# Other DMA engines and smaller pieces for the 352 uneven rows of `w_out` in a memory-bound decode kernel

## The chip, the cores and the metric

The kernel runs on one core of a Trainium2 chip. The metric is the device time of one execution in microseconds; three runs of the kernel before the change gave 663.13, 663.26 and 663.29 us, a median of 663.26 us.

## What is computed

One decode step for four sequences: a layer norm, attention over a cache of 4096 keys and values in 32 heads of 128, and beside it a gated MLP (gMLP) that reads the same normed input. Cut to what matters:

```
xn  = layernorm(x)                                   # (4, 1, 640)
q   = xn @ wq                                        # wq 640 x 4096, 32 heads of 128
o   = softmax(q k^T / sqrt(128)) v                   # k, v: 4 x 32 x 4096 x 128, bf16
A   = o @ wo                                         # wo 4096 x 640
z   = gelu(xn @ w_in)                                # w_in 640 x 1728
g   = w_sp * layernorm(z[864:]) + b_sp
B   = (z[:864] * g) @ w_out                          # w_out 864 x 640
out = x + A + B
```

The two caches are 134 MB each, and all other tensors together 14 MB; nearly everything the kernel does is to read the caches once.

## The kernel before

**The stream.** All big loads are DMAs issued by the sync engine (SP) in the order in which they stand in the program: `wq` (L111), `w_in` (L114), the first 512 rows of `w_out` (L118), the other 352 rows of `w_out` in four DMAs (L128), then 16 units of keys and 16 units of values (L167, 8 MB each, some cut in two), and between and behind them `wo` (L175). A unit is 128 partitions x 64 KB. The units are placed in five slots of one big tile `kv`; a load into a slot waits until the engines that read the slot's last content are done. A DMA of 128 partitions is spread over the core's 16 DMA engines, eight partitions to each. Each engine has its own queue and works it off in order.

**The 352 rows.** 864 rows of `w_out` are 512 + 352. The 512 go four to a partition over all 128 partitions (`w_out`, FA = 4). The 352 are put into `w_rest`, nine chunks (FR = 9) of up to 44 partitions. The table `RB` has an entry for each DMA: the quarter of 32 partitions, the first chunk, a number of engines `ni`, and a number of rows per partition `n`. A DMA gets 4 x `ni` partitions with `n` consecutive rows of 1280 B in each. Its source is written with the dimension `ni` outermost, and so it runs on `ni` DMA engines: 8 and 5 for the first quarter, 3 and 3 for the second. In rows per engine that is 68 on engines 0 to 2, 32 on engines 3 and 4, 28 on engines 5 to 7, none on 8 to 15.

**Semaphores of DMAs.** The framework gives the DMAs that SP and ACT issue eight semaphores in turn, in program order: the three small loads of ACT (L105, L107, L108) and SP's own share them. A DMA that gets a semaphore which an earlier DMA used waits, on the issuing engine, until that earlier DMA has landed whole. The eight are called HW0 to HW7 here.

**The MLP.** After `w_in` has landed, TensorE computes `z` (L309 for the 512 rows' part, L312 for the rest, one matmul for each quarter and each of DC = 5 chunks), ACT applies gelu (L318, and L322 with two instructions for each entry of `RB`), a short chain over DVE, POOL and ACT makes the gated vector `uT` (L353), and 26 matmuls at L367 multiply it with `w_out` and `w_rest`.

**The attention.** For each eighth of a key unit, DVE transposes 128 x 2048 words into a tile `kT` (L389, two buffers in turn, from the pool `ktpool`) and TensorE makes scores from it (L400). The two buffers of `ktpool` first hold `w_rest`, so the first transposes wait for the matmuls of L367. After the softmax, values are multiplied at L474. The end is a projection with `wo` (L517) whose last pieces are loaded last, one sum on DVE (L580), and the store of the result (L583).

Of the kernel before, what the change touches and what calls it, by code (L numbers as in the profile page):

```python
# [11 lines left out]
F32 = mybir.dt.float32  # L12
BF16 = mybir.dt.bfloat16
# [3 lines left out]
def kernel(  # L17
# [19 lines left out]
    nc = tc.nc  # L37
    P = 128
    B, Sq, D = A_x.shape
    _, H, Sk, Dh = A_k_cache.shape  # L40
# [4 lines left out]
    NE = HG // HP  # L45
    M = P // HG
    T = Sk // M
    C2 = 2
    TC = 32
# [6 lines left out]
    Fh = F2 // 2  # L56
    FA = 4
    FR = 9
    RB = ((0, 0, 8, 7), (0, 7, 5, 1), (1, 0, 3, 7), (1, 7, 3, 2))
    NRP = 44  # L60
    assert Fh == FA * P + 4 * sum(i * c for _, _, i, c in RB)
    FC = FA + FR
    NOUT = A_wo.shape[1]
    NH = 2
    NO2 = NOUT // NH
# [3 lines left out]
    const = ctx.enter_context(tc.tile_pool(name="const", bufs=1))  # L69
    small = ctx.enter_context(tc.tile_pool(name="small", bufs=2))  # L70

    NKT = max(2 * TC * 32, 7 * NOUT // 2)
    ktpool = ctx.enter_context(tc.tile_pool(name="ktpool", bufs=2))
    ppool = ctx.enter_context(tc.tile_pool(name="ppool", bufs=2))
    ps_s = ctx.enter_context(tc.tile_pool(name="ps_s", bufs=1, space=bass.MemoryType.PSUM))
    ps_o = ctx.enter_context(tc.tile_pool(name="ps_o", bufs=2, space=bass.MemoryType.PSUM))
# [6 lines left out]
    def misc_ps(shape, dtype):  # L83
        misc_ctr[0] += 1
        return ps_m.tile(shape, dtype, tag="misc", name=f"misc{misc_ctr[0]}")


    SL = T * Dh // 2
    kv = const.tile([P, 5 * SL], BF16)

    def at_slot(i, n, off=0):
        return kv[:, i * SL + off:i * SL + off + n]
# [20 lines left out]
    w_in = at_slot(2, n_in).rearrange("p (c f) -> p c f", c=DC)  # L113
    nc.sync.dma_start(out=w_in, in_=B_w_in.rearrange("(p c) f -> p c f", c=DC))  # L114

    nf = FA * P
    w_out = at_slot(2, FA * NOUT, n_in).rearrange("p (c n) -> p c n", c=FA)
    nc.sync.dma_start(out=w_out, in_=B_w_out[0:nf, :].rearrange("(p c) n -> p c n", p=P))  # L118
    w_rest = []
    for k, n in ((0, 7), (1, 2)):  # L120
        t = ktpool.tile([P, NKT], F32, tag="kT", name=f"w_rest{k}")[:NRP].bitcast(BF16)[:, 0:n * NOUT]
        w_rest.append(t.rearrange("p (c n) -> p c n", c=n))
    nc.gpsimd.memset(w_rest[1].rearrange("p c n -> p (c n)").bitcast(F32), 0.0)
    r_at = [nf]
    for q, c0, ni, n in RB:
        r_at.append(r_at[-1] + 4 * ni * n)
        k = c0 // 7
        nc.sync.dma_start(out=w_rest[k][32 * q:32 * q + 4 * ni, 0:n].rearrange("p c n -> p (c n)"),  # L128
                          in_=B_w_out[r_at[-2]:r_at[-1], :].rearrange("(r i c) n -> i r (c n)", r=4, c=n))

    NB = 32 * FC
    z_at = n_in + FA * NOUT
# [19 lines left out]
    def unit(item, t0, t1):  # L152

        s0, s1 = place[item]
        assert s1 == s0 + 1 or t1 <= T // 2 or t0 >= T // 2
        if t0 >= T // 2:
            return at_slot(s1, (t1 - t0) * Dh, t0 * Dh - SL)
        return at_slot(s0, (t1 - t0) * Dh, t0 * Dh)
# [91 lines left out]
    for q in range(4):  # L250
        nc.gpsimd.tensor_copy(out=SelE[32 * q:32 * q + 32, :, q % 2, :],
                              in_=b8[32 * q:32 * q + 32, 8:8 + HP, None].to_broadcast((32, HP, P // HG)))
# [10 lines left out]
                          in_=ident_f[:].rearrange("p (q x c) -> p q x c", q=2, c=C2))  # L263
# [10 lines left out]
    proj = ps_j.tile([64, 512], F32)  # L274
    RW = NH * B
    for hf in range(NH):
        nc.tensor.matmul(proj[0:32, 0:NO2], lhsT=ident_bf[:XR, 1 - hf:33 - hf],
                         rhs=x_bf[:, hf * NO2:(hf + 1) * NO2], start=(hf == 0), stop=False)
# [4 lines left out]
    for hf in range(2):  # L283
        for c in range(DC):
            for j in range(NG):
                n0 = j * HG * Dh + hf * 512
                nc.tensor.matmul(q4_ps[32 * j:32 * j + 32, hf * 512:hf * 512 + 512], lhsT=xnT[:, c, :],  # L287
                                 rhs=wq[:, c, n0:n0 + 512], start=(c == 0), stop=(c == DC - 1))
# [13 lines left out]

    w_z = w_in.rearrange("p c (a f) -> p c a f", a=2)
    z_ps = misc_ps([P, 2, FA, 32], F32)
    zr_ps = misc_ps([64, 2, 256], F32)
    w_za = w_z[:, :, :, 0:nf].rearrange("p c a (q j i) -> p c q a i j", q=4, j=32)
    for c in range(DC):
        for q in range(4):
            nc.tensor.matmul(z_ps[32 * q:32 * q + 32], lhsT=xnT[:, c, :], rhs=w_za[:, c, q], start=(c == 0), stop=(c == DC - 1))  # L309
        for q in range(2):  # L310
            f0, f1 = r_at[2 * q], r_at[2 * q + 2]
            nc.tensor.matmul(zr_ps[32 * q:32 * q + 32, :, 0:f1 - f0], lhsT=xnT[:, c, :],  # L312
                             rhs=w_z[:, c, :, f0:f1], start=(c == 0), stop=(c == DC - 1))
    z_f = at_slot(2, 2 * 3 * NB, z_at).bitcast(F32).rearrange("p (a n) -> p a n", a=3)
    z_b = at_slot(2, 2 * NB, z_at + 6 * NB).rearrange("p (a n) -> p a n", a=2)
    zT = z_f[:, 0:2, :].rearrange("p a (i j) -> p a i j", j=32)
    nc.gpsimd.memset(z_f[:, 0:2, :], 0.0)
    nc.scalar.activation(out=zT[:, :, 0:FA, :], in_=z_ps[:], func=ACT.Gelu_apprx_tanh)  # L318
    for (q, c0, ni, n), f0, f1 in zip(RB, r_at[:-1], r_at[1:]):
        f0, f1 = f0 - r_at[2 * q], f1 - r_at[2 * q]  # L320
        for a in range(2):
            nc.scalar.activation(out=zT[32 * q:32 * q + 32, a, FA + c0:FA + c0 + n, 0:4 * ni].rearrange("p c (i r) -> p c i r", r=4),  # L322
                                 in_=zr_ps[32 * q:32 * q + 32, a, f0:f1].rearrange("p (r i c) -> p c i r", r=4, c=n),
                                 func=ACT.Gelu_apprx_tanh)

    one_bf = const.tile([1, P], BF16)
# [27 lines left out]
    uT = z_b[:, 1, :]  # L354
# [6 lines left out]
    for f0 in range(0, FC, 4):  # L361
        for hf in range(NH):
            for fc in range(f0, min(f0 + 4, FC)):
                n = P if fc < FA else NRP
                nb = 32 if fc == 1 and hf == 0 else RW
                u0, r0 = 32 * fc + 1 - hf, 32 * (fc % 2)
                nc.tensor.matmul(proj[r0:r0 + nb, 0:NO2], lhsT=uT[:n, u0:u0 + nb],  # L367
                                 rhs=(w_out[:, fc] if fc < FA else w_rest[(fc - FA) // 7][:, (fc - FA) % 7])[:, hf * NO2:(hf + 1) * NO2],
                                 start=(fc == 1 and hf == 0), stop=False)


# [9 lines left out]
    def emit_K(u, k):  # L381

        g, b = divmod(u, B)
        hh = first.get(u, 0) ^ (k // 4)
        qp, kh = k // 2 % 2, k % 2
        t0 = 2 * TC * (2 * hh + qp)
        kw = unit(("k", u), t0, t0 + 2 * TC).bitcast(F32).rearrange("p (t w) -> p t w", w=KW)[:, :, 32 * kh:32 * kh + 32]
        kT = ktpool.tile([P, NKT], F32, tag="kT", name="kT")[:, 0:2 * TC * 32]
        nc.vector.transpose(kT[:].rearrange("p (t r) -> p t r", r=32), kw)  # L389
        if ("S", g) not in state:  # L390
            S_new = ps_s.tile([P, 2, TC, M], F32, tag="S", name="S")
            state[("S", g)] = S_new
        S_ps = state[("S", g)]
        kb = kT[:].bitcast(BF16).rearrange("p (i t e m w) -> p i t e m w", i=2, e=NE, m=M, w=2)
        w0 = 8 - (b * C2 + hh)
        for w in range(2):
            for i in range(2):
                for e in range(NE):
                    q = 2 * qp + e
                    nc.tensor.matmul(S_ps[32 * q:32 * q + 32, i], lhsT=QZ[:, b, 2 * kh + w, e, w0:w0 + 32],  # L400
                                     rhs=kb[:, i, :, e, :, w], start=(b == 0 and k < 4 and kh == 0 and w == 0),
                                     stop=(b == B - 1 and k >= 4 and kh == 1 and w == 1))
# [124 lines left out]
    for i, item in enumerate(seq):  # L527
        if i + 1 < len(seq):
            key, u = seq[i + 1]
            load_unit(seq[i + 1])  # L530
            if key == "k" and u == 2 * B - 1:
                load_wo(u // B - 1)
        else:
            load_wo(NG - 3)
            load_wo(NG - 2)
            load_wo(NG - 1, (0, 4, 6, 7, 8))
        key, u = item
        g, b = divmod(u, B)
        if key == "k":
            done = b == B - 1 and g > 0  # L540
            for k in range(8):
                emit_K(u, k)
                if done and k == 1:
                    emit_sel(g - 1)
                if done and k == 2:
                    emit_oT(g - 1)
                if done and k == 5 and g == 1:
                    emit_proj(g - 1)
            if b == B - 1:
                if g < NG - 1:  # L550
                    fill_qz(g + 1)
                softmax(g)
        else:
            emit_V(u)
# [6 lines left out]
    for c, hf in ((0, 0), (1, 0), (0, 1), (1, 1), (2, 0), (2, 1)):  # L561
        p = min(c, 1)
# [49 lines left out]
```

## Time and profile before

| | |
|---|---|
| median of three runs | 663.26 us |
| profiled execution, span from first to last instruction | 661.2 us |
| outside the span (median less span) | 2.0 us |
| bytes read from HBM | 282.24 MB, 427 GB/s over the span |
| busy: PE, DVE, ACT, POOL | 287.5, 372.2, 73.6, 67.0 us |
| chain that ended last: DMA, DVE, PE | 77%, 9%, 4% |
| packets on SP's queue (q1) | 6879, 99.0% of 16 engines' span |
| instruction packets on q8 | 17, 0.28 MB |

The page gives the profiled execution's span; the run's own time is 2.0 us longer because of what lies around the first and the last instruction. "DMA" shares are means over 16 engines. "SPq" rows are SP's queue: the time it took to issue a DMA, with the wait ahead of it where several are merged in one row. The trace also keeps each DMA packet with its start, length and size, though not the number of its engine.

### The profile page before, as it was taken

The page shows a single profiled execution, that of the slowest core. Times are in us where ns is not written, and L with a number is a line of the kernel's source. Part 1 is how long each engine was busy: PE and PEld are TensorE (multiplying, and loading weights), DVE is VectorE, ACT ScalarE, POOL GpSimd, SP SyncE. Part 2 cuts the span into 40 slices and gives each one's busy share as a digit, 9 for nine tenths or more (in the row PEclk, how much of TensorE's full clock was granted, in tenths as well). Part 3 has the DMA queues.
Part 4 walks back from the last instruction along what each step waited for, and adds up shares of the span by engine and source line. Part 5 has one row for each costly group of instructions (what it writes and reads, how often), then busy time and mean ns, then how long its engine had stood idle before and what let it go on. Part 6 is the DMA issues. An engine that isn't in the chain of part 4 may idle for free.

```text
span 661.2 us, 5415 instructions
## 1 busy us (share of the span) xinstructions
PE 287.5 (43%) x2247; PEld 106.6 (16%) x2247; DVE 372.2 (56%) x306; ACT 73.6 (11%) x145; POOL 67.0 (10%) x137
## 2 busy tenths in 40 slices
PE   0436656446062555235436065533706244551236
PEld 0211212112011121111112022110202112120113
DVE  2229999766191759718356286764629175971112
ACT  0300000341100000430200000070110000043200
POOL 3600000031200000130300000030110000003300
PEclk9857788669577587676758577875858769766678
DMA  9999999999999999999999999999999999999996
GB/s 372 452 446 420 420 447 438 429 444 417 436 436 433 428 425 437 433 436 445 416 432 433 432 421 450 427 432 429 437 440 433 424 433 416 445 444 429 419 420 285
DMA packets 6930, 282.58 MB, mean 427 GB/s; under 512 B 811, under 2 KB 1091, under 8 KB 1487
## 3 DMA queue, kind: packets, MB, share of 16 engines
q1 hardware_dynamic: 6879, 282.24, 99.0%
q8 instruction: 17, 0.28, 0.2%
q14 instruction: 6, 0.05, 0.0%
q10 hardware_dynamic: 28, 0.01, 0.0%
HBM read 282.24 MB, written 0.01 MB: 427 GB/s over the span
## 4 chain that ended last, share of the span: by engine, by line
DMA 77%; DVE 9%; issue 8%; PE 4%; ACT 0%; SPq 0%; DVEq 0%; ACTq 0%
DMA kv<-in_A_k_cache_dram 46%; DMA kv<-in_A_v_cache_dram 26%; DVE kT L389 8%; PE O L474 4%; DMA kv<-in_A_wo_dram 4%; DMA kv<-in_A_wq_dram 2%; DVE pT_t L456 0%; ACT Zb L437 0%; DVE m L407 0%; ACT p_bf L450 0%; PE S L400 0%; PE misc L411 0%; SPq L128 0%; PE proj L517 0%; DVE o_q L569 0%
## 5 line engine op out<-in xcount | busy, mean ns | idle before, releaser
L389 DVE STREAM_TRANSPOSE kT<-kv 128x2048 f32<-128x2048 f32 x128 | 282.8, 2275 | 128.1 <-DMA kv<-in_A_k_cache_dram 128.1
L400 PE MATMUL S<-kT,QZ 128*32 128x512 bf16 x1024 | 187.1, 498 | 261.9 <-DVE kT L389 261.9
L400 PEld LDWEIGHTS <-QZ 128*32 128x32 bf16 x1024 | 59.8, 110 | 387.5 <-issue 323.2
L474 PE MATMUL O<-kv,Zb 128*32 128x512 bf16 x1024 | 75.0, 458 | 56.4 <-DMA kv<-in_A_v_cache_dram 49.5
L437 ACT ACTIVATE Zb<-pT_t,MkE 32x128 bf16<-32x128 bf16 x120 | 60.8, 507 | 117.6 <-PE O L474 104.6
L483 DVE TENSOR_TENSOR om<-O,Mk 128x512 f32<-128x512 f32 x15 | 10.4, 692 | 93.8 <-PE O L474 93.8
L435 POOL TENSOR_SCALAR Zb<-pT_t,MkE 32x128 bf16<-32x128 bf16 x60 | 43.1, 718 | 138.6 <-PE O L474 126.1
L474 PEld LDWEIGHTS <-Zb 128*32 128x32 bf16 x1024 | 34.0, 113 | 97.3 <-issue 69.6
L450 ACT ACTIVATE p_bf<-S,negmax 128x1024 bf16<-128x1024 f32 x4 | 4.5, 1115 | 403.7 <-DVE negmax L417 403.7
L433 DVE TENSOR_SCALAR Zb<-pT_t,MkE 32x128 bf16<-32x128 bf16 x76 | 25.1, 330 | 2.3
L375 POOL COPY QZ<-qT 32x32 bf16<-32x32 bf16 x16 | 5.0, 315 | 188.9 <-PE S L400 188.4
L484 DVE TENSOR_REDUCE R<-om 128x128 f32<-128x512 f32 x15 | 15.3, 1021 | 0.5
L456 DVE STREAM_TRANSPOSE pT_t<-p_bf 128x1024 bf16<-128x1024 bf16 (+1 forms) x8 | 9.6, 1240 | 5.5 <-ACT p_bf L450 5.5
L461 POOL TENSOR_SCALAR rs<-MkB,rowsum 128x4 f32<-128x4 f32 x4 | 1.2, 299 | 112.7 <-ACT p_bf L450 112.7
L507 POOL MEMSET oT<- 128x66 bf16 x4 | 0.5, 146 | 96.6 <-PE proj L517 96.6
L407 DVE TENSOR_REDUCE m<-S 128x1 f32<-128x1024 f32 x4 | 4.9, 1224 | 6.0 <-PE S L400 6.0
L486 DVE TENSOR_SCALAR R<-O,Mk 128x128 f32<-128x128 f32 x1 | 0.3, 350 | 14.0 <-PE O L474 14.0
L496 PE MATMUL misc<-R,SelX 128*128 128x512 f32 x8 | 4.5, 644 | 7.2 <-DVE R L484 5.5
L287 PE MATMUL q<-kv,xnT 128*32 128x512 bf16 x40 | 4.3, 614 | 6.4 <-DVE xnT L208 6.4
L463 PE MATMUL misc<-rs,SelE 128*128 128x4 f32 x8 | 2.4, 365 | 10.4 <-POOL rs L461 10.4
L191 DVE CAST kv<-kv 8x640 f32<-8x640 bf16 x1 | 0.5, 482 | 10.7 <-DMA kv<-in_A_x_dram 10.7
L499 DVE TENSOR_TENSOR om<-misc,h 128x512 f32<-128x512 f32 x4 | 2.8, 692 | 4.9 <-PE misc L496 4.9
(102 smaller groups left out, 80.0 us busy)
## 6 DMA issues: line engine op xcount, KB each, us to landing
kv<-in_A_k_cache_dram SPq DMA_DIRECT2D x8, 4096.0 KB, 30.5
kv<-in_A_v_cache_dram SPq DMA_DIRECT2D x1, 6144.0 KB
kv<-in_A_wq_dram SPq DMA_DIRECT2D x1, 5120.0 KB
kv<-in_A_wo_dram SPq DMA_DIRECT2D x3, 1280.0 KB
kv<-in_B_w_in_dram SPq DMA_DIRECT2D x1, 2160.0 KB, 19.8
kv<-in_A_v_cache_dram SPq DMA_DIRECT2D x1, 2048.0 KB
kv<-in_B_w_out_dram SPq DMA_DIRECT2D x1, 640.0 KB, 20.9
kv<-in_A_wo_dram SPq DMA_DIRECT2D x1, 640.0 KB
```

The lines of the kernel that those rows point to most:

```text
L375: nc.gpsimd.tensor_copy(out=QZ[r0:r0 + 32, :, :, :, 8 + 8 * hp], in_=qT[32 * g:32 * g + 32, NE * hp:NE * hp + NE].rearrange("p e a b -> p ...
L389: nc.vector.transpose(kT[:].rearrange("p (t r) -> p t r", r=32), kw)
L400: nc.tensor.matmul(S_ps[32 * q:32 * q + 32, i], lhsT=QZ[:, b, 2 * kh + w, e, w0:w0 + 32], rhs=kb[:, i, :, e, :, w], start=(b == 0 and k < ...
L407: nc.vector.tensor_reduce(out=m1[:], in_=S_ps[:].rearrange("p i t m -> p (i t m)"), axis=AX.X, op=ALU.max)
L433: nc.vector.tensor_scalar(out=dst, in0=src, scalar1=mk, scalar2=None, op0=ALU.mult)
L435: nc.gpsimd.tensor_scalar(out=dst, in0=src, scalar1=mk, scalar2=None, op0=ALU.mult)
L437: nc.scalar.activation(out=dst, in_=src, func=ACT.Copy, scale=mk)
L450: nc.scalar.activation(out=p_bf[:, M:M + NP], in_=S_ps[:].rearrange("p i t m -> p (i t m)"), func=ACT.Exp, bias=negmax[:, 0:1], scale=scal ...
L456: nc.vector.transpose(pT_t[:, j0:j1, :], blocks)
L474: nc.tensor.matmul(O_ps[32 * q:32 * q + 32, :, :], lhsT=Zb[b % 2][:, w].rearrange("p h c -> p (h c)"), rhs=vv[:, w * 4 * Dh:(w + 1) * 4 * ...
L483: nc.vector.tensor_tensor(out=om4[:], in0=O_ps[:], in1=Mk4[:, :, None].to_broadcast((P, 4, Dh)), op=ALU.mult)
L484: nc.vector.tensor_reduce(out=R, in_=om4[:].rearrange("p c d -> p d c"), axis=AX.X, op=ALU.add)
```

## The change

The 352 rows are cut otherwise. The table `PC` has eight entries (quarter, first partition in it, engines `k`, partitions per engine `r`, first chunk, chunks `n`), each one DMA with `k` as the outermost dimension of its source:

| DMA | engines | rows on each | bytes of a packet |
|---|---|---|---|
| 1 | 0-4 | 4 x 8 | 10240 |
| 2 | 0-2 | 4 x 9 | 11520 |
| 3 | 0-8 | 1 | 1280 |
| 4 | 0-1 | 1 | 1280 |
| 5 | 0-6 | 4 | 1280 |
| 6 | 0-1 | 2 x 5 | 6400 |
| 7 | 0-14 | 1 | 1280 |
| 8 | 0-9 | 1 | 1280 |

In rows per engine: 86 on engines 0 and 1, 75 on 2, 39 on 3 and 4, 7 on 5 and 6, 3 on 7 and 8, 2 on 9, 1 on 10 to 14, none on 15.

With it: `w_rest` is spread over all four quarters of partitions and lies in one tile `kT_t` with two halves, which replaces the two buffers of `ktpool` (`kT_t[:, k % 2]` for the transposes); the whole of `w_rest`, 128 x 2880 words, is set to zero on DVE ahead of its DMAs, where POOL set 44 x 640 words to zero; L312 has four matmuls for each chunk where it had two; L322 has 16 gelu instructions where it had 8; the matmuls of L367 read 128 rows where those on `w_rest` read 44.

```diff
-    RB = ((0, 0, 8, 7), (0, 7, 5, 1), (1, 0, 3, 7), (1, 7, 3, 2))
+    PC = ((0, 0, 5, 4, 0, 8), (1, 0, 3, 4, 0, 9), (1, 16, 9, 1, 0, 1), (1, 25, 2, 1, 0, 1), (2, 0, 7, 4, 0, 1), (2, 28, 2, 2, 0, 5),
+          (3, 0, 15, 1, 0, 1), (3, 16, 10, 1, 0, 1))
...
-    ktpool = ctx.enter_context(tc.tile_pool(name="ktpool", bufs=2))
...
+    kT_t = const.tile([P, 2, NKT], F32)
...
-    nc.gpsimd.memset(w_rest[1].rearrange("p c n -> p (c n)").bitcast(F32), 0.0)
...
-    for q, c0, ni, n in RB:
...
-        nc.sync.dma_start(out=w_rest[k][32 * q:32 * q + 4 * ni, 0:n].rearrange("p c n -> p (c n)"),
-                          in_=B_w_out[r_at[-2]:r_at[-1], :].rearrange("(r i c) n -> i r (c n)", r=4, c=n))
+    w_words = kT_t[:].rearrange("p i n -> p (i n)")[:, 0:FR * NOUT // 2]
+    nc.vector.memset(w_words, 0.0)
...
+    for (q, x0, k, r, c0, n), f0, f1 in zip(PC, f_at[:-1], f_at[1:]):
+        p0 = 32 * q + x0
+        nc.sync.dma_start(out=w_rest[p0:p0 + k * r, c0:c0 + n].rearrange("p c n -> p (c n)"),
+                          in_=B_w_out[f0:f1, :].rearrange("(r i c) n -> i r (c n)", i=k, c=n))
...
-        for q in range(2):
-            f0, f1 = r_at[2 * q], r_at[2 * q + 2]
+        for q, (f0, f1) in enumerate(fq):
             nc.tensor.matmul(zr_ps[32 * q:32 * q + 32, :, 0:f1 - f0], lhsT=xnT[:, c, :],
...
-    for (q, c0, ni, n), f0, f1 in zip(RB, r_at[:-1], r_at[1:]):
+    for (q, x0, k, r, c0, n), f0, f1 in zip(PC, f_at[:-1], f_at[1:]):
...
-        kT = ktpool.tile([P, NKT], F32, tag="kT", name="kT")[:, 0:2 * TC * 32]
-        nc.vector.transpose(kT[:].rearrange("p (t r) -> p t r", r=32), kw)
+        kT = kT_t[:, k % 2]
+        nc.vector.transpose(kT.rearrange("p (t r) -> p t r", r=32), kw)
```

More of the change, by code (lines that the diff above doesn't have):

```diff
@@ L58 @@
     FR = 9
-    RB = ((0, 0, 8, 7), (0, 7, 5, 1), (1, 0, 3, 7), (1, 7, 3, 2))
-    NRP = 44
-    assert Fh == FA * P + 4 * sum(i * c for _, _, i, c in RB)
+    nf = FA * P
+    PC = ((0, 0, 5, 4, 0, 8), (1, 0, 3, 4, 0, 9), (1, 16, 9, 1, 0, 1), (1, 25, 2, 1, 0, 1), (2, 0, 7, 4, 0, 1), (2, 28, 2, 2, 0, 5),
+          (3, 0, 15, 1, 0, 1), (3, 16, 10, 1, 0, 1))
+    f_at = [nf]
+    for _, _, k, r, _, n in PC:
+        f_at.append(f_at[-1] + k * r * n)
+    assert Fh == f_at[-1]
     FC = FA + FR
@@ L70 @@
     small = ctx.enter_context(tc.tile_pool(name="small", bufs=2))
-    NKT = max(2 * TC * 32, 7 * NOUT // 2)
-    ktpool = ctx.enter_context(tc.tile_pool(name="ktpool", bufs=2))
+    NKT = 2 * TC * 32
     ppool = ctx.enter_context(tc.tile_pool(name="ppool", bufs=2))
@@ L114 @@
     nc.sync.dma_start(out=w_in, in_=B_w_in.rearrange("(p c) f -> p c f", c=DC))
-    nf = FA * P
     w_out = at_slot(2, FA * NOUT, n_in).rearrange("p (c n) -> p c n", c=FA)
     nc.sync.dma_start(out=w_out, in_=B_w_out[0:nf, :].rearrange("(p c) n -> p c n", p=P))
[L119 to L122, printed above, removed]
-    nc.gpsimd.memset(w_rest[1].rearrange("p c n -> p (c n)").bitcast(F32), 0.0)
-    r_at = [nf]
-    for q, c0, ni, n in RB:
-        r_at.append(r_at[-1] + 4 * ni * n)
-        k = c0 // 7
-        nc.sync.dma_start(out=w_rest[k][32 * q:32 * q + 4 * ni, 0:n].rearrange("p c n -> p (c n)"),
-                          in_=B_w_out[r_at[-2]:r_at[-1], :].rearrange("(r i c) n -> i r (c n)", r=4, c=n))
+    w_words = kT_t[:].rearrange("p i n -> p (i n)")[:, 0:FR * NOUT // 2]
+    nc.vector.memset(w_words, 0.0)
+    w_rest = w_words.bitcast(BF16).rearrange("p (c n) -> p c n", c=FR)
+    for (q, x0, k, r, c0, n), f0, f1 in zip(PC, f_at[:-1], f_at[1:]):
+        p0 = 32 * q + x0
+        nc.sync.dma_start(out=w_rest[p0:p0 + k * r, c0:c0 + n].rearrange("p c n -> p (c n)"),
+                          in_=B_w_out[f0:f1, :].rearrange("(r i c) n -> i r (c n)", i=k, c=n))
     NB = 32 * FC
@@ L304 @@
     z_ps = misc_ps([P, 2, FA, 32], F32)
-    zr_ps = misc_ps([64, 2, 256], F32)
+    zr_ps = misc_ps([P, 2, 256], F32)
+    fq = [(min(f_at[i] for i in range(len(PC)) if PC[i][0] == q), max(f_at[i + 1] for i in range(len(PC)) if PC[i][0] == q))
+          for q in range(4)]
     w_za = w_z[:, :, :, 0:nf].rearrange("p c a (q j i) -> p c q a i j", q=4, j=32)
@@ L318 @@
     nc.scalar.activation(out=zT[:, :, 0:FA, :], in_=z_ps[:], func=ACT.Gelu_apprx_tanh)
-    for (q, c0, ni, n), f0, f1 in zip(RB, r_at[:-1], r_at[1:]):
-        f0, f1 = f0 - r_at[2 * q], f1 - r_at[2 * q]
+    for (q, x0, k, r, c0, n), f0, f1 in zip(PC, f_at[:-1], f_at[1:]):
+        f0, f1 = f0 - fq[q][0], f1 - fq[q][0]
+        rows = slice(32 * q, 32 * q + 32)
         for a in range(2):
-            nc.scalar.activation(out=zT[32 * q:32 * q + 32, a, FA + c0:FA + c0 + n, 0:4 * ni].rearrange("p c (i r) -> p c i r", r=4),
-                                 in_=zr_ps[32 * q:32 * q + 32, a, f0:f1].rearrange("p (r i c) -> p c i r", r=4, c=n),
+            nc.scalar.activation(out=zT[rows, a, FA + c0:FA + c0 + n, x0:x0 + k * r].rearrange("p c (i r) -> p c i r", r=r),
+                                 in_=zr_ps[rows, a, f0:f1].rearrange("p (r i c) -> p c i r", r=r, c=n),
                                  func=ACT.Gelu_apprx_tanh)
@@ L363 @@
             for fc in range(f0, min(f0 + 4, FC)):
-                n = P if fc < FA else NRP
                 nb = 32 if fc == 1 and hf == 0 else RW
                 u0, r0 = 32 * fc + 1 - hf, 32 * (fc % 2)
-                nc.tensor.matmul(proj[r0:r0 + nb, 0:NO2], lhsT=uT[:n, u0:u0 + nb],
-                                 rhs=(w_out[:, fc] if fc < FA else w_rest[(fc - FA) // 7][:, (fc - FA) % 7])[:, hf * NO2:(hf + 1) * NO2],
+                nc.tensor.matmul(proj[r0:r0 + nb, 0:NO2], lhsT=uT[:, u0:u0 + nb],
+                                 rhs=(w_out[:, fc] if fc < FA else w_rest[:, fc - FA])[:, hf * NO2:(hf + 1) * NO2],
                                  start=(fc == 1 and hf == 0), stop=False)
@@ L393, in emit_K @@
         S_ps = state[("S", g)]
-        kb = kT[:].bitcast(BF16).rearrange("p (i t e m w) -> p i t e m w", i=2, e=NE, m=M, w=2)
+        kb = kT.bitcast(BF16).rearrange("p (i t e m w) -> p i t e m w", i=2, e=NE, m=M, w=2)
         w0 = 8 - (b * C2 + hh)
```

## The prediction

> **What bounds the kernel now.** I read the page first: its DMA rows, then the chain that ended last.
>
> ```profile
> span 661.2 us, 5415 instructions
> ...
> DMA  9999999999999999999999999999999999999996
> ...
> q1 hardware_dynamic: 6879, 282.24, 99.0%
> q8 instruction: 17, 0.28, 0.2%
> ...
> DMA 77%; DVE 9%; issue 8%; PE 4%; ACT 0%; SPq 0%; DVEq 0%; ACTq 0%
> ```
>
> No slice but the last has idle DMA engines. The windows by time, second, show how the stream ends (the last two columns are the DMA share and GB/s):
>
> ```profile
> 620.00:655.00 35.00, 13.95 (x146) 5.96 (x147) 4.82 (x8) 0.00 (x0) 0.00 (x0) 0.67 0.98 417
> 655.00:656.00 1.00, 0.99 (x16) 0.70 (x16) 0.26 (x2) 0.00 (x0) 0.00 (x0) 1.00 0.77 303
> 656.00:657.00 1.00, 0.70 (x12) 0.40 (x10) 0.00 (x0) 0.00 (x0) 0.00 (x0) 1.00 0.53 200
> 657.00:658.00 1.00, 1.00 (x19) 0.61 (x14) 0.66 (x2) 0.00 (x0) 0.00 (x0) 1.00 0.19 69
> ```
>
> The 16 engines run dry one after another; the last decides. To see which, I followed the packet records engine by engine (a packet starts 3 to 4 ns before its predecessor on the engine ends, and the order of sizes is known). No engine ever idles for want of an issued load; the largest gap after 18 us is 0.2 us. A 65536 B packet takes 2.42 us on every engine. Engines differ by two things: the uneven rows, and the 17 instruction packets of q8, which come in a fixed turn over eight engines and delay one by about 1.5 us each:
>
> | engines | uneven rows | q8 packets | last packet ends, us |
> |---|---|---|---|
> | 0-2 | 68 | 0 | 657.15, 657.30, 657.64 |
> | 3, 4 | 32 | 0 | 655.28, 656.63 |
> | 5-7 | 28 | 0, 2, 2 | 654.64, 657.59, 657.62 |
> | one of 8-15 | 0 | 3 | 657.73 |
> | five of 8-15 | 0 | 2 | 656.27 to 656.42 |
> | two of 8-15 | 0 | 0 | 653.44, 654.11 |
>
> I call the engine with three q8 packets X. Behind its 657.73 come the last matmuls, L580 and the store (L583 is issued at 658.92), 3.5 us to the end of the span, and 2.0 us outside of it: 663.26.
>
> Third, SP's queue at the start and the chain beside it:
>
> ```profile
> 0.71 0.39 SPq L111 DMA_DIRECT2D kv<-in_A_wq_dram  x1
> 1.17 0.41 SPq L114 DMA_DIRECT2D kv<-in_B_w_in_dram  x1
> 1.62 0.46 SPq L118 DMA_DIRECT2D kv<-in_B_w_out_dram  x1
> 2.12 14.46 SPq L128 DMA_DIRECT2D w_rest<-in_B_w_out_dram  x4
> 16.62 0.41 SPq L167 DMA_DIRECT2D kv<-in_A_k_cache_dram  x1
> ```
> ```profile
> 0.71 15.13 DMA kv<-in_A_wq_dram
> 15.84 0.02 issue
> 15.86 0.72 SPq L128
> 16.58 0.04 issue
> 16.62 28.44 DMA kv<-in_A_k_cache_dram
> ```
> ```profile
> L128 SPq DMA_DIRECT2D w_rest<-in_B_w_out_dram x4: 719/779/881, 2.1 to 15.9; - x4
> ```
>
> The fourth uneven DMA stands at the head of SP's queue until `wq` has landed (15.84): the DMAs share eight semaphores, and by the built program it gets HW1, which `wq` had. The first key load follows at 16.62. The engines work on `wq` to 14.5-15.5, on `w_in` to 19.6-20.6, on `w_out` to 21.2-21.5 (one to 22.17), so it was queued 4.6 us before any needed it.
>
> **The change part by part.**
>
> *Four more DMAs in the ring of eight semaphores.* In the built programs the turn is: ACT's three small ones HW0, 2, 3; `wq` HW1; `w_in` HW4; `w_out` HW5. Before, the uneven DMAs got HW6, 7, 0, 1 and the first key load HW2, which a two-byte load had: no wait. After, they get HW6, 7, 0, 1, 2, 3, 4, 5, and the first key load gets HW6. So the seventh waits until `w_in` has landed, the eighth until `w_out` has, and the key load behind them until the first uneven DMA has. Only then does SP issue any more work for engines that end `w_out` at 21.3.
>
> Times: an increment comes 0.35 us after the last packet (15.491 to 15.84 for `wq`). `w_in` lands at 20.62 + 0.35 = 20.97, `w_out` at 22.17 + 0.35 = 22.52. The eighth issues in 0.72 to 0.88 us: 23.2 to 23.4. The first uneven DMA follows `w_out` on engines 0-4, four packets of 10240 B at 0.381 us from row to row: 21.46 + 1.53 + 0.35 = 23.33. The key load issues at 23.4; it was 16.62. Behind it the next key load waits for HW7, free at 25.1, which 19 us of queued keys cover.
>
> From issue to full flow: the out store's first packet starts 0.82 us after its issue; `wq`'s first packets start 1.0 to 1.4 us after its issue and take 0.5 to 0.9 us longer than 1.51, in sum 1.8 to 2.0 on most engines. A key load into 16 empty queues is nearer to `wq`, but in a warm kernel: I take 1.5, with 0.8 and 2.0 as ends. So X goes on with keys at 23.4 + 1.5 = 24.9 where it did at 21.26: +3.64 us (2.9 to 4.2). Its own new piece, one row of 0.05 us, lies in the gap.
>
> One rule of the Trainium skill bears on that term. "DMA: Bandwidth & Descriptors", section "Specifications", gives about 0.6 us to the first byte for loads issued by SP. The rows here show 0.82 at the least; by the page the term would be 23.4 + 0.6 - 21.26 = 2.7 us.
>
> *More and fewer rows.* Per row 0.0477 us in the big packets, 0.051 in the 1280 B ones, 0.006 for each DMA's end. Engines 0 and 1 get 4.17 us where they had 3.29 (+0.88), 2 gets +0.34, 3 and 4 +0.36, 5 and 6 -0.96, 7 -1.17. Engines 0-2 have work beyond 24.9, so for them these shifts are all: 658.0 to 658.5. Engines 3 to 7 run dry at 21.4 to 23.2 and then start keys at 24.9, 2.1 to 2.3 later than before: at most 659.9. The rest of 8-15 end at 656.4 + 3.6 = 660.0. X is last: 657.73 + 3.64 = 661.4, and the 3.5 us behind it follow.
>
> The same skill page, section "Latency and other measured facts", says that engines 7 and 15 are usually slower than the others. That would speak for relieving them; the 2.42 us on all 16 here does not show it.
>
> *The memset on DVE*, 2880 words on 128 partitions: POOL's 640 took 0.62 us, so about 3 us at that rate; DVE has nothing to do until 10.7. It ends long before 15.84. Cover gone: at most 3 us of SP's start, and still none of the stream.
>
> *Eight more gelus and ten more z matmuls*: 8 x 0.19 + 10 x 0.39 / 4 (four overlap) = 2.5 us at most in the chain to L367, which ended at 39.3; the first transpose is at 45.25, 5.9 us later. Without that cover the transposes of key unit 0 are late by the excess, and the load into its slot (issued 54.2, needed at 63) still has 9 us. Matmuls with 128 rows instead of 44 cost nothing: 0.47 us in both rows of L367. `kT_t` keeps two buffers: the built program's transposes still wait for the scores two steps back.
>
> Sum: 663.26 + 3.64 = **666.9 us**.
>
> **The rivals.** (1) *No gap*: the key load is at the engines in time, because one of the waits is not where I see it. It decides as soon as it issues before 20.5 instead of 23.4. Then X gets 0.06 us and engines 0 and 1 end at 658.0 to 658.5: +0.3 to +0.8, 663.5 to 664.1, no change that counts. For it: in before the gap does not exist with the same ring; against it: the `wq` wait of 11.2 us is plainly there and works by the same turn. Chance 0.08. (2) *A gap, and X not the last*: the turn of q8 packets starts elsewhere and X is among engines 0 to 7. Then another of 8-15, with two packets, ends at 660.0, and X among 5-7 at 659.9 + 1.5 = 661.4; among 0-4 at most 660.3. The time is 665.5 to 666.9. Chance 0.07. (3) *A second stall*: the start shifts and a later load misses its slot. Covers are 9 us and more at the second and third key loads; the price is that of a late load, 1 to 3 us above my sum: 668 to 670. Chance 0.05. (4) Faster at all needs X earlier, and nothing in the change moves it earlier but fewer q8 packets; ten more matmul pairs make more, not fewer. Chance 0.01.
>
> **How the numbers follow.** The forecast, 0.79, gives 2.9 to 4.2 us, 666.2 to 667.5. The bounds with rival 2 below and half of rival 3 above give 665.5 to 668.0, with less than 2 in 10 left out. A measurement of this kernel can tell about 0.2% (1.3 us) from none. Slower by more: the forecast and rivals 2 and 3, 0.91. Within: rival 1, 0.08. Faster: 0.01.
>
> **What would show it.** SP's rows after: the eighth uneven DMA starts at about 22.5, the first key load at about 23.4. The DMA share falls below half between 22 and 24.5 us. The engines' last packets lie between 658 and 661.5, X alone at the end. A key load at 17 us, or a DMA row without a hole there, makes the prediction wrong.

## The result, and the profile after

The changed kernel takes 667.94 us (median of 5 runs, 667.80 to 668.66) beside 663.28 us (5 runs, 663.13 to 663.34): 4.66 us more, a ratio of 1.0069 with an interval of 1.0057 to 1.0081. The profiled execution has a span of 666.0 us where the one before had 661.2 us. In the experiments further below, one run of 777.85 us (pad_all), far above its 11 others, is left out of the median.

The page of the changed kernel: span, DMA row, the two queues of the stream, and the chain that ended last.

```profile
span 666.0 us, 5451 instructions
...
DMA  8999999999999999999999999999999999999996
...
q1 hardware_dynamic: 6937, 282.24, 98.4%
q8 instruction: 17, 0.28, 0.2%
...
DMA 74%; DVE 12%; issue 11%; PE 2%; ACT 0%; DVEq 0%; SPq 0%; ACTq 0%
```

The bytes and the instruction packets are the same, and the DMA row hides the loss: a slice is 16.65 us, a packet counts where it starts, and the first digit moved only from 0.91 to 0.90. The page's GB/s row shows more: 396 in the second slice where it had 452. SP's queue in the timeline of the changed kernel (start, us, engine, line, operation):

```profile
0.72 0.40 SPq L117 DMA_DIRECT2D kv<-in_A_wq_dram  x1
1.18 0.41 SPq L120 DMA_DIRECT2D kv<-in_B_w_in_dram  x1
1.63 0.46 SPq L123 DMA_DIRECT2D kv<-in_B_w_out_dram  x1
3.87 19.08 SPq L130 DMA_DIRECT2D kT_t<-in_B_w_out_dram  x8
23.61 32.81 SPq L169 DMA_DIRECT2D kv<-in_A_k_cache_dram  x3
```

The eight uneven DMAs end at 3.87 + 19.08 = 22.95, and the first key load goes out at 23.61, where it went out at 16.62. SP's waits in the first 60 us of the same kernel say on what (engine and line, what it waited for, us in total, times, longest):

```profile
...
SPq L130 <- DMA kv<-in_A_wq_dram: 9.9, 1, 9.9
SPq L130 <- DMA kv<-in_B_w_in_dram: 3.3, 1, 3.3
SPq L169 <- DMA kT_t<-in_B_w_out_dram: 2.0, 2, 1.4
SPq L130 <- DVE kT_t L125: 1.8, 1, 1.8
SPq L130 <- DMA kv<-in_B_w_out_dram: 1.2, 1, 1.2
```

The three loads of the ring stand there by name: `wq`, then `w_in`, then `w_out`; and the key load itself waits for an uneven DMA (the shorter of its two waits, 2.0 - 1.4 = 0.6 us, lies ahead of the first key load). The chain that ended last, in order of time, now begins with these pieces (start, us, what):

```profile
0.71 0.67 issue
1.39 2.47 DVE kT_t L125
...
3.87 19.72 DMA kT_t<-in_B_w_out_dram
23.60 0.02 issue
23.61 23.23 DMA kv<-in_A_k_cache_dram
```

The key load is released at 23.59 by the landing of the first uneven DMA, issued at 3.87. (The memset in the chain only sets when that DMA is issued. On the engines it lies behind `w_out` and moves no earlier without the memset.) The windows by time show the hole and the end (the last two columns are the DMA share and GB/s; a packet counts where it starts):

```profile
22.00:23.00 1.00, 1.00 (x34) 0.98 (x29) 0.65 (x1) 0.32 (x1) 0.83 (x5) 1.00 0.47 155
23.00:24.00 1.00, 0.74 (x14) 0.35 (x5) 0.70 (x1) 0.56 (x2) 1.00 (x6) 1.00 0.25 92
24.00:25.00 1.00, 0.00 (x0) 0.03 (x1) 0.55 (x1) 0.99 (x1) 0.57 (x5) 1.00 2.33 784
...
659.00:660.00 1.00, 0.41 (x6) 0.28 (x7) 0.24 (x2) 0.00 (x0) 0.00 (x0) 1.00 0.58 224
661.00:662.00 1.00, 0.89 (x14) 0.59 (x15) 0.14 (x1) 0.00 (x0) 0.00 (x0) 1.00 0.06 24
```

A DMA share of 0.47 and 0.25 in two slices that were full before; 2.33 in the third, because eleven of the engines start a 65536 B packet in it; and at 661 us a share of 0.06, which is one engine of 16.

The packet records, put together engine by engine as for the prediction, give this for X (the engine with three q8 packets):

| engine X | before | after | forecast |
|---|---|---|---|
| key load issued, us | 16.62 | 23.61 | 23.4 |
| first key packet starts | 21.256 | 24.789 | |
| that packet takes, ns | 2418 | 3298 | |
| last packet ends | 657.73 | 662.27 | 661.4 |

X ends 4.54 us later, and what follows it follows as before. The two last steps of the timeline of the changed kernel:

```profile
663.12 0.32 DVE L583 TENSOR_TENSOR o_bf<-last,o_q 64x160 bf16<-64x160 f32 x1
663.47 0.32 SPq L586 DMA_DIRECT2D out_dram<-o_bf  x1
```

The store goes out at 663.47 where it went out at 658.92: +4.55.

### The profile page after: what moved, and what is told of

It is laid out like the page before. It is cut to its first block, busy times and chain, and to the rows that moved or that the text cites. A ratio compares the mean times of both kernels' runs of the same rounds, so it can differ in the third digit from the quotient of the medians.

```text
span 666.0 us, 5451 instructions
## 1 busy us (share of the span) xinstructions
PE 281.9 (42%) x2257; PEld 106.5 (16%) x2257; DVE 374.7 (56%) x307; ACT 74.3 (11%) x153; POOL 66.3 (10%) x136
## 4 chain that ended last, share of the span: by engine, by line
DMA 74%; DVE 12%; issue 11%; PE 2%; ACT 0%; DVEq 0%; SPq 0%; ACTq 0%
DMA kv<-in_A_k_cache_dram 63%; DVE kT_t L392 10%; DMA kv<-in_A_v_cache_dram 5%; DMA kv<-in_A_wo_dram 4%; DMA kT_t<-in_B_w_out_dram 3%; PE O L477 1%; DVE kT_t L125 0%; DVE pT_t L459 0%; DVE Zb L436 0%; PE S L403 0%; DVE m L410 0%; ACT p_bf L453 0%; PE proj L520 0%; DVE o_q L572 0%; PE misc L414 0%
## 5 line engine op out<-in xcount | busy, mean ns | idle before, releaser
L392 DVE STREAM_TRANSPOSE kT_t<-kv 128x2048 f32<-128x2048 f32 x128 | 282.8, 2274 | 128.8 <-DMA kv<-in_A_k_cache_dram 128.7
L403 PE MATMUL S<-kT_t,QZ 128*32 128x512 bf16 x1024 | 181.4, 486 | 266.6 <-DVE kT_t L392 266.6
L520 PE MATMUL proj<-kv,oT 128*8 128x320 bf16 x54 | 5.6, 350 | 1.5 <-DMA kv<-in_A_wo_dram 1.5
```

Source lines behind the costliest of these rows:

```text
L392: nc.vector.transpose(kT.rearrange("p (t r) -> p t r", r=32), kw)
L520: nc.tensor.matmul(dst[0:nb, 0:n1 - n0], lhsT=state[("oT", g)][:, c0:c0 + nb], rhs=wo_t[g][:, c, n0:n1], start=start, stop=stop)
```

## The experiments

**The theory and its rivals.** The theory is that of the prediction: the ring of eight semaphores holds the key load back, the engines run empty, and X carries the gap to the end. The rivals: the other edits of the change (memset, gelus, matmuls, one tile for two buffers) cost something; or the new distribution of rows costs something by itself.

### Two-byte DMAs alone: dummy1, dummy2, dummy3, dummy4

The kernel before, with n DMAs of two bytes each added behind the four uneven ones on SP's queue (n = 1, 2, 3, 4). They take places in the ring and move nothing. `dm` is used nowhere.

```diff
+    dm = const.tile([1, 8], BF16)
+    for j in range(n):
+        nc.sync.dma_start(out=dm[:, j:j + 1], in_=B_w_sp)
```

> The kernel before, with one two-byte DMA more on SP's queue between the uneven DMAs and the first key load. Theory RING (the wait for a semaphore of the ring of eight decides): the key load gets HW3, which the small load of x had; it has landed at 10.7 us, so there is no wait. The key load issues at about 17.4 us, no engine idles, 663.3 us. Theory LOAD (more rows on the lowest engines and more small packets decide): 663.3 as well, since two bytes are no load. This run is the foot of the ladder.

> The kernel before with two two-byte DMAs more. RING: the key load gets HW4 and waits until w_in has landed, at about 21.0 us; with 2.06 us from issue to full flow, as in the changed kernel, engine X starts keys 1.8 us later than in the kernel before: 665.1 us. LOAD: 663.3.

> The kernel before with three two-byte DMAs more. RING: the key load gets HW5 and waits until w_out has landed, at about 22.5 us; X is 3.3 us later: 666.6 us. LOAD: 663.3.

> The kernel before with four two-byte DMAs more: as many DMAs as the changed kernel has, on the old rows. RING: the fourth waits for w_out (22.5 us) and is issued in 0.7 us, the key load gets HW6 and waits for the first uneven DMA (23.2): issue at 23.3, X 4.1 us later, 667.4 us; nearly the whole of the changed kernel's 4.66 us. LOAD: 663.3.

| kernel | key load issued, us | median, us (runs) | over before (663.33) | ratio and interval |
|---|---|---|---|---|
| dummy1 | 16.98 | 663.41 (10) | +0.08 | 1.0003 (0.9991 to 1.0015) |
| dummy2 | 21.11 | 665.89 (7) | +2.56 | 1.0035 (1.0023 to 1.0047) |
| dummy3 | 22.46 | 666.71 (5) | +3.38 | 1.0038 (1.0019 to 1.0056) |
| dummy4 | 23.32 | 667.67 (4) | +4.34 | 1.0059 (1.0039 to 1.0078) |

SP's queue in dummy2, then in dummy4, and SP's waits in dummy4:

```profile
16.76 0.70 SPq L133 DMA_DIRECT2D dm<-in_B_w_sp_dram  x2
21.11 33.86 SPq L171 DMA_DIRECT2D kv<-in_A_k_cache_dram  x3
```
```profile
16.92 6.09 SPq L133 DMA_DIRECT2D dm<-in_B_w_sp_dram  x4
23.32 32.86 SPq L171 DMA_DIRECT2D kv<-in_A_k_cache_dram  x3
```
```profile
SPq L133 <- DMA kv<-in_B_w_in_dram: 3.6, 1, 3.6
...
SPq L133 <- DMA kv<-in_B_w_out_dram: 1.3, 1, 1.3
...
SPq L171 <- DMA w_rest<-in_B_w_out_dram: 0.3, 1, 0.3
```

This is a ladder with the rungs of the ring. One more DMA costs nothing. With the second, the key load itself gets the semaphore of `w_in`; with the third, that of `w_out`; with the fourth, that of the first uneven DMA. Eight bytes in all cost 4.34 us. Dummy4 issues its key load 0.29 us ahead of the changed kernel (23.32 against 23.61), and 4.34 + 0.29 = 4.63 is, within the spread of dummy4's four runs (667.08 to 668.55), the 4.66 of the change. So the four further DMAs give the whole loss. Where the 0.8 us above the expectation come from in dummy2 is told further below, with the term from issue to full flow.

### The rest of the change without the further DMAs: old_rows

The changed kernel with the four DMAs of before in the new table.

```diff
-    PC = ((0, 0, 5, 4, 0, 8), (1, 0, 3, 4, 0, 9), (1, 16, 9, 1, 0, 1), (1, 25, 2, 1, 0, 1), (2, 0, 7, 4, 0, 1), (2, 28, 2, 2, 0, 5),
-          (3, 0, 15, 1, 0, 1), (3, 16, 10, 1, 0, 1))
+    PC = ((0, 0, 8, 4, 0, 7), (0, 0, 5, 4, 7, 1), (1, 0, 3, 4, 0, 7), (1, 0, 3, 4, 7, 2))
...
-          for q in range(4)]
+          for q in range(2)]
```

> The changed kernel (one tile kT_t, zeros set on DVE, loops over the table) with the old four DMAs in its table: 68 rows on engines 0 to 2, 32 on 3 and 4, 28 on 5 to 7, and half as many gelus. RING: no wait ahead of the first key load, 663.3 us. A theory that the other edits cost (memset on DVE, one tile for both buffers): 667.9.

663.39 us (12 runs) beside 663.39: ratio 1.0002 (0.9991 to 1.0013). The key load is issued at 16.75. The memset on DVE, the tile `kT_t` and the wider matmuls cost nothing. The eight further gelus and the ten further matmuls for `z` are not in this kernel, since they go with the table; that the dummies alone make the whole loss says that they cost nothing either.

### The same rows in five DMAs: five_dmas

The same rows on the same engines as in the changed kernel, but for a few; with five DMAs, the first key load gets a semaphore that is free early.

```diff
+    PC = ((0, 0, 5, 4, 0, 8), (1, 0, 3, 4, 0, 9), (2, 0, 7, 4, 0, 1), (2, 28, 2, 2, 0, 5), (3, 0, 9, 2, 0, 2))
```

> The changed kernel with its rows per engine nearly kept (86 on engines 0 and 1, 76 on 2, 40 on 3 and 4, 8 on 5 and 6, 4 on 7 and 8) in five DMAs instead of eight. RING: the key load gets HW3, which is free; no gap; the rows alone remain: engines 0 and 1 end 0.9 us later than before and take over as the last, 0.3 to 0.8 us behind X: 663.6 to 664.1 us. LOAD: near the changed kernel, 667.9.

664.83 us (11 runs) beside 663.39: ratio 1.0015 (1.0006 to 1.0024). The key load is issued at 17.56, no engine idles, and 3.2 us of the loss are gone (4.66 less 1.44). But 1.44 us stay, 0.7 us more than the upper end of the expectation.

### The same eight DMAs with a key load among them: keys_between

```diff
+    load_rest(0, 2)
     load_unit(seq[0])
+    load_rest(2, len(PC))
```

`load_rest(a, b)` issues the uneven DMAs a to b - 1; the loop at L130 is taken out.

> The changed kernel with all its eight DMAs as they are, but the first key load is issued after the second of them, and the six small ones behind it. RING: the key load gets HW0, which a two-byte load had; no gap at 21 us. The six small pieces land after key unit 0, so the matmuls of L367 and with them the first transposes start later (near 48 us instead of 45), which the 9 us ahead of the third key load cover. Only the rows remain: 663.6 to 664.1 us. LOAD: 667.9, since every row and packet is there.

SP's queue in keys_between:

```profile
3.87 1.75 SPq L131 DMA_DIRECT2D kT_t<-in_B_w_out_dram  x2
5.66 0.41 SPq L170 DMA_DIRECT2D kv<-in_A_k_cache_dram  x1
15.94 7.67 SPq L131 DMA_DIRECT2D kT_t<-in_B_w_out_dram  x6
```

664.76 us (11 runs) beside 663.39: ratio 1.002 (1.0011 to 1.0029). All packets are those of the changed kernel and SP still waits to 23.61; but the engines have 8 MB of keys by then, and 3.3 us of the loss are gone. Again about 1.4 us stay.

So the gap is settled, and the rows have a price of their own that was not forecast. I measured it as a rate: for each us, the usual duration of the packets under way (2418 ns for 65536 B, 338 for 8960) over the one they took. It is 1.00 in the kernel before from 12 to 34 us. In five_dmas it is 0.90, 0.87, 0.83, 0.77, 0.76, 0.89 and 0.96 in the seven us from 22 on, on all 16 engines, those without a row of `w_out` too; what these and the 0.97 of the us before lack to 1 is 1.05 us. X ends at 659.01, 1.28 later than before, and the engines with the most rows some 0.4 us behind it. In keys_between the rate is 0.99 or more until 40 us, and falls to 0.82 from 44 to 46, when the pieces issued behind the key load pass. Something in the pieces slows all engines.

### Where the pieces land: old_rows_upper

Two theories. PLACE: a piece that an engine writes to partitions other than those it writes in the ordinary loads slows all engines. STEP: where the piece is written does not matter. The kernel is old_rows with the four DMAs of before, the same engines and the same packets, written to the quarters 2 and 3 of the partitions and not to 0 and 1.

```diff
-    PC = ((0, 0, 8, 4, 0, 7), (0, 0, 5, 4, 7, 1), (1, 0, 3, 4, 0, 7), (1, 0, 3, 4, 7, 2))
+    PC = ((2, 0, 8, 4, 0, 7), (2, 0, 5, 4, 7, 1), (3, 0, 3, 4, 0, 7), (3, 0, 3, 4, 7, 2))
...
-          for q in range(2)]
+          for q in range(2, 4)]
...
-        for q, (f0, f1) in enumerate(fq):
+        for q, (f0, f1) in enumerate(fq, 2):
...
-        f0, f1 = f0 - fq[q][0], f1 - fq[q][0]
+        f0, f1 = f0 - fq[q - 2][0], f1 - fq[q - 2][0]
```

The last three edits let the matmuls for `z` and the gelus of these rows follow to the same quarters.

> Five DMAs and the keys-between order cost 1.4 us without any gap: in both, the 65536 B packets of all engines took 2.6 to 3.2 us instead of 2.42 around the small pieces. What is open is why. This run is the changed kernel with the old four DMAs, their destination moved from the lower to the upper 64 partitions; every engine's rows and the order stay. Theory PLACE (engines 0 to 7 write where the others write, and that slows all): the same slow phase, 664.4 to 665 us. Theory STEP (engines work through the key rows in a settled order of phases, and shifting some of them against the others unsettles it): nothing is shifted otherwise than before, 663.4 us.

666.71 us (5 runs, 666.59 to 666.84) beside 663.39: ratio 1.0046 (1.0033 to 1.0059). The windows from 24 to 28 us of old_rows, then of old_rows_upper:

```profile
24.00:28.00 4.00, 0.16 (x1) 0.03 (x1) 1.47 (x4) 3.80 (x11) 2.68 (x9) 0.94 1.01 436
```
```profile
24.00:28.00 4.00, 0.19 (x2) 0.05 (x1) 1.32 (x4) 3.93 (x11) 2.43 (x6) 1.00 0.82 230
```

436 GB/s against 230 (the last column), with nothing changed but the destination of the pieces and the quarters of the arithmetic that follows them. The packets of 8960 B that took 338 ns take up to 715, and the key packets of the engines without a piece take 4.2 to 4.8 us and not 2.42. The rate is 0.52 to 0.60 from 22 to 28 us; from 21 to 31 it lacks 3.30 us, and the time is 3.32 longer. PLACE holds and STEP falls, though PLACE's own figure, 664.4 to 665, was 1.7 us too low.

### Pieces into an unused tile: pad_seven, pad_nine, pad_all, pad_all_plain

old_rows with a fifth DMA from `w_out` into a tile `pad` that nothing reads: 28 rows that engines 0 to 6 write to their own partitions; 9 rows, one on each of engines 0 to 8; and 128 rows, eight on each engine, cut in two ways. In pad_all engine i writes the partitions 8i to 8i + 7; in pad_all_plain the same eight packets of 1280 B go to the places of an ordinary load.

```diff
+    pad = const.tile([P, NOUT], BF16)
+    # pad_seven
+    nc.sync.dma_start(out=pad[0:28, :], in_=B_w_out[0:28, :].rearrange("(r i c) n -> i r (c n)", i=7, c=1))
+    # pad_nine
+    nc.sync.dma_start(out=pad[0:9, :], in_=B_w_out[0:9, :].rearrange("(r i c) n -> i r (c n)", i=9, c=1))
+    # pad_all
+    nc.sync.dma_start(out=pad[0:128, :], in_=B_w_out[0:128, :].rearrange("(r i c) n -> i r (c n)", i=16, c=1))
+    # pad_all_plain
+    nc.sync.dma_start(out=pad[:], in_=B_w_out[0:128, :])
```

> The changed kernel with the old four DMAs and a fifth that copies 28 rows into an unused tile, four 1280 B packets on each of engines 0 to 6, ahead of the first key load; no gap in the ring of eight. STEP: engines 0 to 6 are shifted by 0.21 us against the others; if that unsettles the order, the packets of keys slow down for some us as in the five-DMA run, 664.2 to 664.8 us. PLACE and plain load: engines 0 to 2 end 0.2 us later, 663.3 to 663.6.

> As the seven-engine pad, but one 1280 B packet on each of engines 0 to 8: a shift of 0.06 us, and engine 8 with it, which had none before. STEP: a slow phase if so small a shift suffices, up to 664.8; PLACE and plain load: 663.4.

> As the seven-engine pad, but eight 1280 B packets on all 16 engines: all are shifted alike, by 0.41 us. STEP: no slow phase, 663.8 us. A theory that small packets ahead of the keys slow the keys whatever their place: 664.8 or more.

> As the pad on all 16 engines, but written as an ordinary load of 128 partitions, as w_out itself is, so that each engine writes the partitions that it writes in every other load; the same eight 1280 B packets on each engine, the same 0.41 us. The pad of before spread engine i over partitions 8i to 8i+7, and cost 0.7 us more than its packets. PLACE (the destination decides): no slow phase, 663.8 us. STEP (the shift of 8 to 15 against 0 to 7 unsettles the order of the key packets, whatever the destination): the slow phase stays, 664.5 us.

pad_seven: 663.50 us, ratio 1.0005 (0.9994 to 1.0016); pad_nine: 663.22, 0.9996 (0.9988 to 1.0005); 11 runs each, beside 663.39. Neither shows a slow stretch. pad_all: 664.52 (11 runs) beside 663.39, 1.0017 (1.0007 to 1.0026). pad_all_plain: 663.66 (11 runs) beside 663.42 on another chip, 0.9999 (0.9990 to 1.0008). The windows from 22 to 28 us of pad_all, then of pad_all_plain:

```profile
22.00:28.00 6.00, 2.74 (x35) 1.48 (x27) 2.68 (x4) 4.07 (x12) 4.00 (x16) 1.00 1.01 391
```
```profile
22.00:28.00 6.00, 1.77 (x19) 0.94 (x14) 2.58 (x4) 4.65 (x12) 4.15 (x16) 0.92 1.07 460
```

391 GB/s against 460. In pad_all the rate lacks 0.77 us from 21 to 29 us; with eight rows of 0.051 that each engine has more, 0.41, that makes 1.18, and 1.13 was measured. In pad_all_plain the rate is 1.00 throughout and the key packets take 2418 ns. The two intervals of the ratio just touch, so the traces carry this verdict more than the times do. PLACE holds again: STEP had 663.8 for pad_all and 664.5 for pad_all_plain, and both came out the other way. The expectation's other rival, that small packets ahead of the keys slow them whatever their place, falls with pad_all_plain too. The pair leaves one thing open: in pad_all an engine also reads rows of `w_out` that lie 16 apart, in pad_all_plain rows that follow one another. In old_rows and old_rows_upper the rows read are the same, so the large effect there is not from the source.

## Why the prediction was right, and which term was too small

**The range.** The order of the waits, the gap and X as the last engine came as forecast. The size did not quite: the forecast by itself had 2.9 to 4.2 us and at most 667.5, and 4.66 us and 667.94 were measured. The time lies within the stated range, just under its upper bound of 668.0, because half of rival 3 had been added on top. Rival 3, a second stall, did not come, so that the bound held is luck; two of the five runs lie above it.

**The ring.** Every wait fell where the prediction put it: `wq`, `w_in`, `w_out`, then the first uneven DMA ahead of the key load. The issue was forecast for 23.4 and came at 23.61. The 0.2 us are in one engine: the last of its four 10240 B packets ended at 23.28 (22.894 + 0.385), so it began the four at about 21.75, where the working took the start from 21.46. The ladder of dummies shows that nothing else is needed for the loss, and old_rows that a key load at 16.75 ends it.

**The rows.** The other engines were forecast to end before X, at 660.0 at the latest, and do end before it: seven at 657.6 to 658.5, eight at 660.3 to 660.8, X at 662.27 alone. Those eight are up to 0.8 us late, which is about what the issue (0.2) and the term below (0.56) add. So where the rows lie is hidden in the changed kernel.

**Memset, gelus, matmuls.** The memset took 2.46 us, beside nothing that mattered. The first transpose came at 47.06 where it had come at 45.25, behind the keys that landed at 46.84 (23.61 + 23.23 in the chain), so neither gelus nor matmuls held it. No DMA engine idles later for want of a load, which is what rival 3 needed. All of this was costed at nothing, and the end moved by 4.55 us, X's 4.54.

**From issue to full flow.** This is the term that failed in size: 1.5 us, with ends of 0.8 and 2.0, from the out store and the start of `wq`. Measured on X it is 1.18 us from the issue to the first packet (23.61 to 24.789) and 0.88 us by which that packet is longer than 2418 ns: 2.06 us, 0.56 more than taken and just past the upper end. The forecast's 3.64, 0.21 for the issue and 0.56 here make 4.41 of X's 4.54; the last 0.13 lie in its later packets. Why I sized it so: of `wq`'s two parts, 1.0 to 1.4 us and 0.5 to 0.9, I let a warm kernel shorten the sum, and nothing shortened it. (The store's first packet starts 0.80 us after its issue, 659.715 against 658.92, and not 0.82; nothing rests on the difference.) The 0.6 us to the first byte that the Trainium skill gives ("DMA: Bandwidth & Descriptors", section "Specifications") were not seen; 2.7 us for the whole shift by it would have been further off.

The long first packets do not come from PLACE alone. Dummy4 has the old rows at the old places, and its rate after the gap is 0.80 at 25 us, 0.81 at 26 and 0.87 at 27, its first key packet on X 3418 ns; the changed kernel has 0.81, 0.82 and 0.83. In dummy2 X's first key packet takes 3451 ns and the one behind it 2667; in dummy3 first key packets take up to 3387. That is part of what dummy2's expectation lacked: X ended at 660.02 there, 2.29 later than before, and three other engines later still, at 660.42 to 660.44. So key packets that start after a gap are slow for three to six us, foreign pieces or not. Why is open.

**Rival 1, no gap**, did not come, but its price was put too low: 663.5 to 664.1 by counting rows. five_dmas and keys_between, which are that case, took 664.83 and 664.76. What the count of rows lacked is the slowing of all engines by pieces in foreign places. In the changed kernel these pieces run in the hole, where most engines are empty, so their share there can't be told from that of the restart; that dummy4, which has none of them, makes 4.63 of the 4.66 us leaves little room for it.

**No version was faster** than the kernel before. X, which has no uneven row, ended last there, at 657.73, with engines 0 to 2 and two of 5 to 7 within 0.6 us of it; X has no uneven row to give away.

## What to carry to other kernels

Count the DMAs between two big loads against the ring of semaphores: a two-byte DMA too many makes the next big load wait for a load far ahead of it, so issue the next big load before the small ones. Ask which engine ends the stream before moving work among the others. When a piece is given to chosen engines, let each write the partitions that it writes in the ordinary loads.

## What was not expected of the hardware

**The place of a piece slows all 16 engines.** The rows in pieces that lie, wholly or in part, outside the writing engine's own partitions, and the time over the kernel before: 9 rows (pad_nine) nothing, about 84 rows (five_dmas, keys_between) +1.4 us, 128 rows (pad_all) +1.1, of which 0.4 are the packets themselves, 352 rows (old_rows_upper) +3.3; in the last the stream falls to 223 GB/s at the lowest us, from 434 in the kernel before. Engines with no such row are slowed as much. The Trainium skill ("DMA: Bandwidth & Descriptors", section "The descriptor swizzle") says which partitions an engine writes in a load of 128 partitions: engine 0 the partitions 0 to 3 and 32 to 35, engine 8 those from 64 and from 96, and so on in fours. The runs agree: four-partition pieces for engines 0 to 7 in quarters 0 and 1 are free, in quarters 2 and 3 they are not. Why foreign writes slow the other engines was not measured.

**A restart is slow.** After a gap, the engines' first 65536 B packets take 2.4 to 4.0 us, most of them over 2.7, where 2418 ns is usual, and the rate is back at 0.98 or more at 28 us (dummy2, dummy4 and the changed kernel).
